# Re-dealing the first batch's k features and masked v between VectorE and ScalarE, with dummy matmuls up to the KV sums

## The chip, the cores and the metric

One core of a Trainium2 chip runs the whole program. The metric is the device time of one execution in microseconds (us). A profiled execution also has a span, from its first to its last instruction; here the time is the span plus 1.8 us (300.69 and 298.9). A change counts as faster or slower from 2% on, which is 6 us here.

## The reference, cut to what matters

Linear attention ("cosformer") over 8 batches, 8 heads, 576 tokens, 64 columns, then a two-layer product with squared ReLU over all 4608 tokens:

```python
q_p = concat([relu(q) * cos_w, relu(q) * sin_w])     # the same for k: 128 features a head
kv  = einsum('bhsf,bhsd->bhfd', k_p, v)              # the "KV sums"
num = einsum('bhsf,bhfd->bhsd', q_p, kv)
x   = num / (einsum('bhsf,bhf->bhs', q_p, k_p.sum(2)) + 1e-6)
out = relu(x @ w_in)**2 @ w_out                      # 512 -> 2048 -> 512
```

## The kernel before: the parts concerned

The products with w1 (`w_in`) and w2 (`w_out`) fill TensorE for most of the time. Only the head of the program, until batch 0's x exists, leaves TensorE free; it then proceeds in slots, in which attention of the next batches is woven into the products. k and v of batch 0 come over SyncE's queue, nine tokens a partition (`J9 = 9`), two halves of the heads in even and odd partitions. v is therefore copied twice per head, masked by half (`half_of`), to bf16 (`v9`, on VectorE, ScalarE or GpSimd):

```python
def of_half(eng, dst, src, g):
    if eng is nc.scalar:
        eng.activation(out=dst, in_=src, func=ACTF.Copy, scale=half_of[:, g : g + 1])
    else:
        eng.tensor_scalar_mul(out=dst, in0=src, scalar1=half_of[:, g : g + 1])
...
with tc.manual_schedule():
    for nm, h0, h1 in (("k", 0, 2), ("k", 2, 4), ("v", 0, 2), ("v", 2, 3), ("v", 3, 4)):
        load_nine(nm, h0, h1, nc.sync)
    load_qa(nc.sync)
    ...
    warm(26)                                  # dummy matmuls
    for h in range(HH):
        k9_dve(h, cos_col, 0)                 # VectorE: k cosine features
    k9_act(0, 2)                              # ScalarE: sines of heads 0 and 1
    k9_dve(2, sin_col, D)
    for g in range(2): v9(dve, 0, g)
    k9_dve(3, sin_col, D)
    for g in range(2): v9(act, 1, g)
    v9(nc.gpsimd, 2, 1, J9 - 1, J9)           # GpSimd: 64 elements; the loads below queue behind it
    load_w1(0, 4); load_qb(nc.gpsimd)         # w1, w2: cast to bf16 on the way, in quarters
    for i in range(1, 4): load_w1(i, 4)
    load_batch(1, nc.gpsimd, "q")
    load_w2(0, 4)
    load_batch(1, nc.gpsimd, "kv"); load_tail("q", 0, nc.gpsimd)
    for i in range(1, 4): load_w2(i, 4)
    ...
    for h in range(HH):
        kv9(h)                                # KV sums, TensorE
        if h == 1: kvz_copy(act, 0, 0, kzs[0][0][:, 0])
        if h > 1:  fill(4)                    # dummy matmuls
    qa_feat(0); kvz_copy(dve, 0, 1, kzs[0][1][:, 0]); qa_feat(1)
    ...
```

(cuts are marked; some short loops are set on one line). All loads by GpSimd are one stream in program order, and its place in GpSimd's program, behind a piece of masked v, is what sets its start. In batch 0's product with w2 each of 16 row blocks is used by four matmuls in turn, so the second quarter of w2 is first read by the 17th matmul.

Of the kernel before, what the change touches and what calls it, by code (L numbers as in the profile page):

```python
# [19 lines left out]
def kernel(  # L20
# [9 lines left out]
    nc = tc.nc  # L30
    P = nc.NUM_PARTITIONS
    B, H, S, D = q.shape
# [6 lines left out]
    J = S // P  # L39
# [24 lines left out]
    J9 = S // TAIL  # L64
    QA = J * TAIL

    def buf_of(nm, b):
        if (nm, b) not in kqv:
            kqv[nm, b] = inp.tile([P, HH * S * D // TAIL], F32, name=nm, tag=nm, bufs=2)
        return kqv[nm, b]  # L70
# [8 lines left out]
    def nine_of(nm):  # L79
        return buf_of(nm, 0).rearrange("p (h j d) -> p h j d", h=HH, j=J9)  # L80
# [24 lines left out]
    def load_rows(dst, src, n, h0, h1, eng):  # L105

        for g in range(2):
            eng.dma_start(  # L108
                out=dst.rearrange("(p g) h j d -> p g h j d", g=2)[:, g, h0:h1],
                in_=src[g * HH + h0 : g * HH + h1].rearrange("h (p j) d -> p h j d", j=n),  # L110
            )

    def load_nine(nm, h0, h1, eng):
        load_rows(nine_of(nm), srcs[nm][0], J9, h0, h1, eng)
# [19 lines left out]
    CA, CB, C9 = J + 1, 2 * J + 1, 2 * J + 3  # L134
    NC = C9 + J9
    cos_col = const.tile([P, NC], F32, name="cos_col")
    sin_col = const.tile([P, NC], F32, name="sin_col")
# [69 lines left out]
    vexts = att.tile([P, 2, J9 * HH, E1], BF16, name="vext")  # L207
# [14 lines left out]
    def vext_of(b, j):  # L222
        return vexts[:, b % 2, j * H : (j + 1) * H, :]

    def vext9(h):
        return vexts[:, :, h * J9 : (h + 1) * J9, :]

    def of_half(eng, dst, src, g):
        if eng is nc.scalar:
# [4 lines that stand above are left out]
    kps, kvzs, kzs, qps, tqs, qpTs, xs = {}, {}, {}, {}, {}, {}, {}  # L234
    nums, rdens, xts, xtails, xTs = {}, {}, {}, {}, {}

    def cached(tiles, key, shape, tag, bufs):
        if key not in tiles:
            tiles[key] = att.tile(shape, BF16, name=tag, tag=tag, bufs=bufs)
        return tiles[key]  # L240
# [8 lines left out]
    def kp9():  # L249
        t = cached(kps, 0, [P, J9 * HH, F], "kp", 1)  # L250
        return t.rearrange("p (h j) f -> p h j f", h=HH)
# [48 lines left out]
            nc.vector.tensor_copy(out=vext_of(b, j)[:, :, 0:D], in_=piece("v", b, j))  # L300


    def k9_dve(h, w, f0):
        nc.vector.scalar_tensor_tensor(  # L304
            out=kp9()[:, h, :, f0 : f0 + D],
            in0=nine_of("k")[:, h, :, :],
            scalar=0.0,
            in1=w[:, C9:NC].unsqueeze(2).to_broadcast([P, J9, D]),
            op0=ALU.max,
            op1=ALU.mult,  # L310
        )

    def k9_act(h0, h1):
        for j in range(J9):
            nc.scalar.activation(
                out=kp9()[:, h0:h1, j, D:F],
                in_=nine_of("k")[:, h0:h1, j, :],
                func=ACTF.Relu,
                scale=sin_col[:, C9 + j : C9 + j + 1],
            )  # L320

    def v9(eng, h, g, j0=0, j1=J9):
        of_half(eng, vext9(h)[:, g, j0:j1, 0:D], nine_of("v")[:, h, j0:j1, :], g)



# [1 line left out]
    def kv9(h):  # L328
        a, c = h // 2, h % 2 * 2 * E1
        if 0 not in kzs:  # L330

            kzs[0] = [
                ps_a.tile([P, 2, FP], F32, name="kz", tag="pa", bufs=1),
                ps_h.tile([P, 2, FP], F32, name="kzh", tag="hps", bufs=2),
            ]
            kvzs[0] = att.tile([P, H, E1], BF16, name="kvz", tag="kvz", bufs=2)
        for j in range(J9):
            nc.tensor.matmul(  # L338
                out=kzs[0][a][:, 0, c : c + 2 * E1].rearrange("p (g e) -> p g e", g=2),
                lhsT=kp9()[:, h, j, :],  # L340
                rhs=vext9(h)[:, :, j, :],
                start=(j == 0 and h % 2 == 0),
                stop=(j == J9 - 1 and h % 2 == 1),
            )

    def kvz_copy(eng, b, a, src):
        copy = eng.copy if eng is nc.scalar else eng.tensor_copy
        copy(
            out=kvzs[b].rearrange("p (g a h) e -> p a h g e", g=2, a=2)[:, a],
            in_=src[:, 0 : HH * E1].rearrange("p (h g e) -> p h g e", h=2, g=2),  # L350
        )

    def warm(n):

        wm = ps_h.tile([P, 2, FP], F32, name="wm", tag="hps", bufs=2)
        for i in range(n):
            nc.tensor.matmul(
                out=wm[:, i % 2, :], lhsT=zeros[:, 0:P], rhs=zeros[:, :], start=True, stop=True
            )

    def fill(n):

        w0 = HH * E1
        for i in range(n):
            nc.tensor.matmul(  # L365
                out=kzs[0][0][:, 0, w0:FP],
                lhsT=zeros[:, 0:P],
                rhs=zeros[:, 0 : FP - w0],
                start=True,
                stop=True,  # L370
            )
# [44 lines left out]
    def qa_feat(t, parts="cs"):  # L416
        for c in parts:
            f = feat_cos if c == "c" else feat_sin
            f(qpa(t), qa_of()[:, :, t, :], CA + t)

    def qa_T(t):
        tq = ps_y.tile([P, HH, P], BF16, name="tqa", tag="yps", bufs=2)
        tqs["a", t] = tq
        for h in range(HH):
            nc.tensor.transpose(tq[:, h, :], qpa(t)[:, h, :], ident[:, :])

    def qa_T_copy(t, eng):
        qpTs["a", t] = att.tile([P, HH, P], BF16, name="qpTp0", tag="qpTp0", bufs=5)
        copy = eng.copy if eng is nc.scalar else eng.tensor_copy
        copy(out=qpTs["a", t][:, :, :], in_=tqs["a", t][:, :, :])  # L430
# [288 lines left out]
    for j in (2, 3):  # L719
# [12 lines left out]
        k=(8, 8, 8, 9, 9),  # L732
        f=(4, 5, 6, 12, 13),
        kv=(10, 10),
        d=(11, 13, 15, 17, 21),
        t=(5, 6, 7, 16, 18),
# [5 lines left out]
        k=(26, 26, 27, 27, 28),  # L742
        f=(18, 20, 22, 26, 26),
        kv=(29, 29),
        d=(30, 31, 32, 33, 34),
# [3 lines left out]
        k=(31, 32, 33, 34, 35),  # L749
        f=(33, 33, 34, 34, 35),  # L750
        kv=(37, 38),
        d=(40, 41, 42, 43, 44),
    )
    for b in range(4, B):
        o, p = second[b - 2], first[b - 1]
# [4 lines left out]
            k=(o, o, o + 1, o + 1, o + 2),  # L760
            f=(o + 4, o + 4, o + 5, o + 5, o + 6),
            kv=(o + 3, o + 4),
            d=[p + 4 + j for j in range(NS)],
# [8 lines left out]
            rest()  # L772

    with tc.manual_schedule():
        for nm, h0, h1 in (("k", 0, 2), ("k", 2, 4), ("v", 0, 2), ("v", 2, 3), ("v", 3, 4)):
            load_nine(nm, h0, h1, nc.sync)
        load_qa(nc.sync)
        constants()
        ones_by_half()
        warm(26)  # L780
        dve, act = nc.vector, nc.scalar
        for h in range(HH):
            k9_dve(h, cos_col, 0)
        k9_act(0, 2)
        k9_dve(2, sin_col, D)
        for g in range(2):
            v9(dve, 0, g)
        k9_dve(3, sin_col, D)
        for g in range(2):
            v9(act, 1, g)  # L790

        v9(nc.gpsimd, 2, 1, J9 - 1, J9)
        load_w1(0, 4)
        load_qb(nc.gpsimd)
        for i in range(1, 4):
            load_w1(i, 4)
        load_batch(1, nc.gpsimd, "q")
        load_w2(0, 4)
        load_batch(1, nc.gpsimd, "kv")
        load_tail("q", 0, nc.gpsimd)  # L800
        for i in range(1, 4):
            load_w2(i, 4)
        load_batch(2, nc.gpsimd, "qkv")
        v9(act, 2, 0)
        v9(act, 2, 1, 0, J9 - 1)
        for g in range(2):
            v9(dve, 3, g)
        for h in range(HH):
            kv9(h)
            if h == 1:  # L810
                kvz_copy(act, 0, 0, kzs[0][0][:, 0])
            if h > 1:
                fill(4)
        qa_feat(0)
        kvz_copy(dve, 0, 1, kzs[0][1][:, 0])
        qa_feat(1)
        qa_T(0)
        qa_T_copy(0, dve)
        qa_feat(2)
        qa_T(1)  # L820
        qa_T_copy(1, dve)
        qa_feat(3)
        fill(2)
        qa_num(0)
        qa_T(2)
        qa_T_copy(2, act)
        fill(2)
        qa_num(1)
        qa_T(3)
        qa_T_copy(3, act)  # L830
        fill(3)
        att_div(0, 0)
        for t in (2, 3):
            qa_num(t)
        att_den(0, 1)
        for t, eng in enumerate((dve, act)):
            xa_T(t)
            xa_copy(t, eng)
        att_mul(0, 1)

        def second_pair():
            for t, eng in ((2, dve), (3, act)):
                xa_T(t)
                xa_copy(t, eng)
            for j in (2, 3):
                att_feat(0, j)

        run(0, {(0, 2): second_pair})
        for s in range(1, len(slots)):
            run(s)  # L850
# [28 lines left out]
```

## Time and profile before

| | before |
|---|---|
| time, median of 3 runs (range) | 301.3 us (300.77 to 301.48) |
| span of the profiled run | 298.9 us |
| TensorE busy | 97% |
| first product with w1 starts | 20.20 us |
| 17th product with w2 starts | 41.85 us |

The prediction shows the lines for this and how they are read.

### The profile page before, as it was taken

What the parts mean: (1) busy time and instruction counts of PE and PEld (TensorE: products, weight loads), DVE (VectorE), ACT (ScalarE), POOL (GpSimd) and SP (SyncE); (2) the same over time, 40 slices, a digit from 0 to 9 for tenths busy, and PEclk for the clock granted to TensorE, in tenths of its full rate; (3) what the DMA queues carried; (4) which work ended last, traced back from release to release, by engine and by line L of the source; (5) the groups of instructions that cost most, each with busy time, mean ns of one, the idle gap of its engine ahead of it and who ended that gap; (6) DMA issues with size and microseconds to landing.
All of it is one profiled execution on the core that took longest, in us unless ns stands there. A gap on an engine that the chain in (4) does not pass through costs nothing.

```text
span 298.9 us, 6467 instructions
## 1 busy us (share of the span) xinstructions
PE 289.2 (97%) x2655; PEld 204.2 (68%) x2677; DVE 144.6 (48%) x357; ACT 154.6 (52%) x229; POOL 50.3 (17%) x87
## 2 busy tenths in 40 slices
PE   8689999999999999999999999999999999999995
PEld 3569855889456984589655884589654884589544
DVE  3777674375649386238740387228740282033100
ACT  5636753666738564555554555555554552155311
POOL 1652504654121002000021001100021000100000
PEclk9799999999999999999999999999999999999999
DMA  6899993999999998799669937799679113100121
GB/s 207 231 235 278 336 203 81 331 329 257 196 195 170 161 311 131 216 199 321 160 154 209 317 62 91 231 185 323 162 158 209 39 35 82 71 35 2 35 72 70
DMA packets 74285, 52.98 MB, mean 177 GB/s; under 512 B 50832, under 2 KB 67984, under 8 KB 74256
## 3 DMA queue, kind: packets, MB, share of 16 engines
q1 hardware_dynamic: 64096, 28.84, 45.6%
q0 software_dynamic: 10016, 23.60, 29.2%
q8 instruction: 21, 0.34, 0.5%
q10 hardware_dynamic: 144, 0.13, 0.1%
q14 instruction: 8, 0.07, 0.1%
HBM read 36.70 MB, written 9.44 MB: 154 GB/s over the span
## 4 chain that ended last, share of the span: by engine, by line
PE 93%; DVE 2%; DMA 2%; ACT 1%; issue 1%; SPq 1%; ACTq 0%; DVEq 0%
PE hps L600 42%; PE yps L639 39%; PE num L514 3%; PE kz L385 2%; PE yh L639 2%; DMA k<-in_k_dram 2%; PE tq L491 1%; SPq L108 1%; PE kz L338 1%; PE kz L396 1%; PE kzh L338 1%; DVE kp L304 1%; PE tx L566 1%; DVE vext L232 1%; PE kz L365 0%
## 5 line engine op out<-in xcount | busy, mean ns | idle before, releaser
L600 PEld LDWEIGHTS <-w1sb 128*128 128x128 bf16 x1312 | 113.4, 98 | 12.7 <-issue 0.6
L600 PE MATMUL hps<-xT,w1sb 128*128 128x256 bf16 (+1 forms) x1056 | 118.3, 269 | 0.6 <-ACT xT L465 0.5
L639 PE MATMUL yps<-w2sb,gT 128*128 128x512 bf16 (+1 forms) x476 | 107.7, 372 | 1.2 <-DVE qpTp L500 0.2
L608 ACT ACTIVATE rt<-hps 128x1024 bf16<-128x1024 f32 x72 | 73.7, 1024 | 57.6 <-DVE gT L615 32.8
L639 PEld LDWEIGHTS <-gT 128*128 128x128 bf16 x528 | 49.8, 98 | 52.7 <-DVE qpTp L500 0.7
L615 DVE TENSOR_TENSOR gT<-rt 128x1024 bf16<-128x1024 bf16 x64 | 44.0, 687 | 79.0 <-ACT rt L608 79.0
L635 POOL DMA_DIRECT2D out_dram<-ysb x36 | 21.0, 584 | 172.5 <-ACT ysb L621 168.0
L621 ACT COPY ysb<-yps 128x512 f32<-128x512 f32 (+1 forms) x35 | 20.0, 575 | 54.0 <-PE yps L639 51.4
L287 ACT ACTIVATE qp<-q,sin_col 128x512 bf16<-128x512 f32 (+1 forms) x34 | 22.3, 693 | 7.5 <-DMA q<-in_q_dram 7.5
L535 DVE TENSOR_TENSOR x<-num,rden 128x512 bf16<-128x512 f32 x32 | 22.1, 691 | 1.1
L287 ACT ACTIVATE kp<-k,sin_col 128x512 bf16<-128x512 f32 (+1 forms) x35 | 21.5, 670 | 0.0
L277 DVE TENSOR_SCALAR qp<-q,cos_col 128x512 bf16<-128x512 f32 (+1 forms) x34 | 15.3, 485 | 11.5 <-DMA q<-in_q_dram 11.5
L528 DVE TENSOR_SCALAR den<-num 128x8 f32<-128x8 f32 (+1 forms) x40 | 6.6, 165 | 22.5 <-PE num L514 21.7
L277 DVE TENSOR_SCALAR kp<-k,cos_col 128x512 bf16<-128x512 f32 (+1 forms) x35 | 15.9, 453 | 0.0
L600 PE MATMUL hps<-xTt,w1sb 128*128 128x128 bf16 x256 | 15.3, 219 | 0.0
L639 PE MATMUL yps<-w2sb,gTt 128*128 128x512 bf16 x64 | 14.5, 379 | 0.0
L514 PEld LDWEIGHTS <-qpT 128*128 128x128 bf16 (+1 forms) x240 | 10.3, 100 | 3.3 <-issue 1.7
L300 DVE CAST vext<-v 128x512 bf16<-128x512 f32 x28 | 11.8, 421 | 0.0
L514 PE MATMUL num<-kvz,qpT 128*128 128x65 bf16 (+1 forms) x240 | 11.7, 194 | 0.0
L639 PEld LDWEIGHTS <-gTt 128*128 128x128 bf16 x64 | 6.3, 98 | 7.5
L385 PEld LDWEIGHTS <-kp 128*128 128x128 bf16 x224 | 8.5, 97 | 2.4
L639 PE MATMUL yh<-w2sb,gT 128*128 128x512 bf16 x30 | 9.1, 379 | 0.1
(80 smaller groups left out, 153.9 us busy)
## 6 DMA issues: line engine op xcount, KB each, us to landing
out_dram<-ysb POOLq DMA_DIRECT2D x26, 256.0 KB, 4.2
k<-in_k_dram SPq DMA_DIRECT2D x4, 1024.0 KB, 6.5
v<-in_v_dram SPq DMA_DIRECT2D x4, 1024.0 KB, 7.5
q<-in_q_dram SPq DMA_DIRECT2D x4, 1024.0 KB, 6.4
q<-in_q_dram POOLq DMA_DIRECT2D x3, 1024.0 KB, 9.9
k<-in_k_dram POOLq DMA_DIRECT2D x3, 1024.0 KB, 10.3
v<-in_v_dram POOLq DMA_DIRECT2D x3, 1024.0 KB, 10.7
w1sb<-in_moe_w_in_dram POOLq DMA_DIRECT2D x4, 512.0 KB, 9.1
```

The lines of the kernel that those rows point to most:

```text
L277: nc.vector.tensor_scalar(out=dst[:, :, 0:D], in0=src, scalar1=0.0, scalar2=cos_col[:, c : c + 1], op0=ALU.max, op1=ALU.mult,)
L287: nc.scalar.activation(out=dst[:, :, D:F], in_=src, func=ACTF.Relu, scale=sin_col[:, c : c + 1])
L300: nc.vector.tensor_copy(out=vext_of(b, j)[:, :, 0:D], in_=piece("v", b, j))
L385: nc.tensor.matmul(out=kz[:, a, c0 : c0 + E1], lhsT=kp_of(b, j)[:, h, :], rhs=vext_of(b, j)[:, h, :], start=(j == 0 and c == 0 and g == 0) ...
L514: nc.tensor.matmul(out=out, lhsT=lhsT, rhs=kvz[:, half * HH + hh, :], start=True, stop=True)
L535: nc.vector.tensor_tensor(out=x_of(b, j).rearrange("p (b k) (l d) -> p b k l d", b=n, l=2), in0=n4[:, :, :, 0:D].rearrange("p b (k l) d -> ...
L600: nc.tensor.matmul(out=out, lhsT=w1sb[:, kb, hb * P : (hb + 1) * P], rhs=rhs, start=(kb == 0), stop=(kb == KB - 1),)
L608: nc.scalar.activation(out=rt[:, :, :], in_=hps[:, :, :], func=ACTF.Relu)
L615: nc.vector.tensor_tensor(out=dst, in0=rt[:, :, :], in1=rt[:, :, :], op=ALU.mult)
L621: nc.scalar.copy(out=ysb[:, c0:c1], in_=acc)
L635: eng.dma_start(out=dst, in_=ysb[p0 : p0 + n, c0:c1])
L639: nc.tensor.matmul(out=acc, lhsT=lhsT, rhs=w2sb[:, hb, c0:c1], start=(hb == 0), stop=(hb == HB - 1))
```

## The change

Its intent: VectorE and ScalarE share k and v more evenly and in larger instructions, so that the KV sums start and end sooner; TensorE runs dummy matmuls right up to them, so that its clock is not lowered; batch 0's query features are computed before the KV sums end. The core of the diff (helpers that only gain an argument are cut):

```diff
-        for nm, h0, h1 in (("k", 0, 2), ("k", 2, 4), ("v", 0, 2), ("v", 2, 3), ("v", 3, 4)):
-            load_nine(nm, h0, h1, nc.sync)
+        for nm in "kv":
+            for h in (0, 2):
+                load_nine(nm, h, h + 2, nc.sync)
...
-        warm(26)
+        warm(34)
...
         k9_act(0, 2)
-        k9_dve(2, sin_col, D)
-        for g in range(2):
-            v9(dve, 0, g)
-        k9_dve(3, sin_col, D)
-        for g in range(2):
-            v9(act, 1, g)
-
-        v9(nc.gpsimd, 2, 1, J9 - 1, J9)
+        k9_act(2, 4, 5)
+        v9(dve, 0, 2, 0)
+        v9(act, 0, 2, 1, 0, 2 * J9 - 2)
+
+        v9(nc.gpsimd, 0, 2, 1, 2 * J9 - 2, 2 * J9)
         load_w1(0, 4)
...
-        v9(act, 2, 0)
-        v9(act, 2, 1, 0, J9 - 1)
-        for g in range(2):
-            v9(dve, 3, g)
+        for h in (2, 3):
+            k9_dve(h, sin_col, D, 5)
+        v9(dve, 2, 4, 0)
+        v9(act, 2, 4, 1)
         for h in range(HH):
             kv9(h)
             if h == 1:
                 kvz_copy(act, 0, 0, kzs[0][0][:, 0])
-            if h > 1:
-                fill(4)
-        qa_feat(0)
-        kvz_copy(dve, 0, 1, kzs[0][1][:, 0])
-        qa_feat(1)
...
+        for t in range(J):
+            qa_feat(t, "c")
+        for t in range(2):
+            qa_feat(t, "s")
+        kvz_copy(act, 0, 1, kzs[0][1][:, 0])
...
```

GpSimd's piece of masked v, ahead of its loads, is now 128 elements of heads 0 and 1, instead of 64 of head 2.

More of the change, by code (lines that the diff above doesn't have):

```diff
@@ L223, in vext_of, with vext9 @@
         return vexts[:, b % 2, j * H : (j + 1) * H, :]
-    def vext9(h):
-        return vexts[:, :, h * J9 : (h + 1) * J9, :]
+    def vext9(h0, h1):
+        return vexts[:, :, h0 * J9 : h1 * J9, :]
     def of_half(eng, dst, src, g):
@@ L300, in att_v, with k9_dve @@
             nc.vector.tensor_copy(out=vext_of(b, j)[:, :, 0:D], in_=piece("v", b, j))
-    def k9_dve(h, w, f0):
+    def k9_dve(h, w, f0, j0=0):
         nc.vector.scalar_tensor_tensor(
-            out=kp9()[:, h, :, f0 : f0 + D],
-            in0=nine_of("k")[:, h, :, :],
+            out=kp9()[:, h, j0:J9, f0 : f0 + D],
+            in0=nine_of("k")[:, h, j0:J9, :],
             scalar=0.0,
-            in1=w[:, C9:NC].unsqueeze(2).to_broadcast([P, J9, D]),
+            in1=w[:, C9 + j0 : NC].unsqueeze(2).to_broadcast([P, J9 - j0, D]),
             op0=ALU.max,
@@ L311, in k9_dve, with k9_act @@
         )
-    def k9_act(h0, h1):
-        for j in range(J9):
+    def k9_act(h0, h1, j1=J9):
+        for j in range(j1):
             nc.scalar.activation(
@@ L320, in k9_act, with v9 @@
             )
-    def v9(eng, h, g, j0=0, j1=J9):
-        of_half(eng, vext9(h)[:, g, j0:j1, 0:D], nine_of("v")[:, h, j0:j1, :], g)
+    def v9(eng, h0, h1, g, i0=0, i1=2 * J9):
+        src = nine_of("v")[:, h0:h1].rearrange("p h j d -> p (h j) d")
+        of_half(eng, vext9(h0, h1)[:, g, i0:i1, 0:D], src[:, i0:i1, :], g)
     def kv9(h):
@@ L340, in kv9 @@
                 lhsT=kp9()[:, h, j, :],
-                rhs=vext9(h)[:, :, j, :],
+                rhs=vext9(h, h + 1)[:, :, j, :],
                 start=(j == 0 and h % 2 == 0),
@@ L811 @@
                 kvz_copy(act, 0, 0, kzs[0][0][:, 0])
-            if h > 1:
-                fill(4)
-        qa_feat(0)
-        kvz_copy(dve, 0, 1, kzs[0][1][:, 0])
-        qa_feat(1)
-        qa_T(0)
-        qa_T_copy(0, dve)
-        qa_feat(2)
-        qa_T(1)
-        qa_T_copy(1, dve)
-        qa_feat(3)
+        for t in range(J):
[3 more added lines that the diff above has]
+        kvz_copy(act, 0, 1, kzs[0][1][:, 0])
+        for t in range(2):
+            qa_T(t)
+            qa_T_copy(t, dve)
+        for t in (2, 3):
+            qa_feat(t, "s")
         fill(2)
```

## The prediction

> **What bounds the kernel now.** I read the page first, for which engine fills the span, then the granted clock, then the chain that ended last over the first 45 us, and last the timeline of GpSimd, which issues the weight loads. Page, busy shares and slices of 7.5 us:
>
> ```profile
> PE 289.2 (97%) x2655; PEld 204.2 (68%) x2677; DVE 144.6 (48%) x357; ACT 154.6 (52%) x229; POOL 50.3 (17%) x87
> ...
> PE   8689999999999999999999999999999999999995
> ...
> DMA  6899993999999998799669937799679113100121
> ```
>
> TensorE is busy in all slices but the first three, so the change, which touches only the first 20 us, can gain only what it moves TensorE's later work forward. The DMA row says that the transfers are as full as TensorE until slice 20: that is the danger. The stretches of the head (columns PE, PEld, DVE, ACT, POOL busy, then granted clock, DMA share and rate):
>
> ```profile
> 10.00:11.00 1.00, 0.00 (x0) 0.00 (x0) 1.00 (x3) 1.00 (x2) 0.91 (x2) 1.00 0.98 320
> ...
> 12.00:13.00 1.00, 1.00 (x12) 1.00 (x11) 1.00 (x2) 0.04 (x1) 1.00 (x2) 0.50 0.54 39
> 13.00:14.00 1.00, 1.00 (x11) 0.94 (x9) 0.37 (x2) 1.00 (x3) 1.00 (x3) 0.50 1.01 164
> ```
>
> TensorE ends its warm matmuls at 8.61, idles 2.45 us, and from 11.4 to 14.8 us works at clock 0.50, just in the KV sums. The chain (start, us, what):
>
> ```profile
> 9.48 1.54 DVE vext L232 x2
> 11.02 0.04 issue
> 11.06 1.87 PE kz L338 x18
> 12.93 0.97 PE kzh L338 x9
> 13.90 0.84 PE kz L365 x4
> 14.74 0.62 PE kzh L338 x9
> 15.38 0.43 DVE kvz L348
> ...
> 20.20 0.61 PE hps L600 x8
> ...
> 41.55 0.43 PE yps L639 x2
> 41.99 0.46 PE yh L639 x2
> ```
>
> The masked v of VectorE releases the KV sums at 11.06; they end at 15.4; the first product with w1 starts at 20.20. Now the loads that GpSimd issues (start, us of issue, what, and what it waited for):
>
> ```profile
> 9.95 0.45 POOL L232 TENSOR_SCALAR vext<-v,half_of 128x64 bf16<-128x64 f32 x1 [8.02 <-DMA v<-in_v_dram]
> 10.48 0.96 POOL L191 DMA_DIRECT2D w1sb<-in_moe_w_in_dram  x1
> ...
> 12.36 2.27 POOL L191 DMA_DIRECT2D w1sb<-in_moe_w_in_dram  x3
> ...
> 20.46 0.63 POOL L92 DMA_DIRECT2D k<-in_k_dram  x1 [1.35 <-DMA w1sb<-in_moe_w_in_dram]
> ...
> 35.35 2.24 POOL L198 DMA_DIRECT2D w2sb<-in_moe_w_out_dram  x3 [2.44 <-DMA k<-in_k_dram]
> ```
>
> From its tenth transfer on GpSimd waits before an issue for the landing of the one eight before it: the stream runs as fast as transfers land, with a DMA share of 1.0 to 1.26 from 13 to 45 us. Landings, as issue plus time to landing: quarters of w1 at 10.48+5.7 = 16.2, 20.2, 23.6 and 13.82+12.3 = 26.1; q for token slots 2 and 3 at 11.44+6.5 = 17.9; the second quarter of w2 at 35.35+6.5 = 41.85. Its first user is the 17th matmul of the product with w2. The third was at 39.01, one takes 0.2165, so it is due at 41.83, and the timeline has it at 41.85, with the chain's piece after it 0.46 instead of 0.43. **This load has no slack.** Quarters 2, 3 and 4 of w1 have 3.1, 1.7 and 1.4 us (users at 23.30, 25.29, 27.50).
>
> **What the Trainium skill says.** (1) "TensorE: Matmul & The Clock Gate", section "What's actually happening": after an idle window of about 3.4 us the array gets half its clock, and a busy one gives it back. The trace agrees in kind: 0.50 for about 3.4 us, though the idle stretch was only 2.45. (2) "VectorE: DVE Perf Modes", section "What auto-detection actually checks": a one-source op in SBUF gets two results a cycle if the outermost dimensions of source and destination are both even, or equal. The trace agrees for even ones: v as 8 x 64 takes 421 ns (batch 1), while the masked copy of one head here, 9 x 64, takes 804. (3) "SBUF — State Buffer", section "Who interferes with whom": VectorE in such a two-port mode and GpSimd take turns at a shared port; the loser waits for the whole instruction. The trace hints at it: query features of 128x256 on VectorE take 344 ns alone and 560 at 15.73, while GpSimd issues. (4) "ScalarE: Activation LUTs", section "What ACT_TABLE_LOAD costs": 186 ns + 0.833 ns an element, 93 more for a pointer operand. Exact here: 386 ns measured at 128, 759 against 764 at 576.
>
> **The change part by part.**
> - Masked v on VectorE: four of 804 ns go, two of 18 x 64 = 1152 come. By (2) they run at two a cycle: the fixed part is 479 - 267 = 212 ns (feature of 512 at 479, 256 cycles at 0.96 GHz), so 600 + 212 = 0.81 us each, the price of one before.
> - k sine features on VectorE: two of 750 ns shrink to 4/9 of their elements. Two-source, 1.04 ns an element: 750 - 320*1.04 = 0.42 each.
> - VectorE: k cosine ends 8.90, v of two heads lands 8.97; v pair 9.05 to 9.86, k sine to 10.6, second v pair (landing about 10.4, estimated from 10.84 before with two issues fewer) to 11.4. Before: 13.1.
> - ScalarE: nine k instructions to 7.6 as before, five more at 0.304 pace to 9.15, v of 1024 elements 1.13 to 10.3, v of 1152 1.24 to 11.4.
> - Eight more warm matmuls at 0.21 = 1.7: TensorE is busy to about 10.3, just where the KV sums can start, with no idle stretch. At full clock one of 130 columns costs 130/2.4 = 54 ns, about 57 (the 65-column ones run at a pace of 31), so 18 take 1.03 instead of 1.87. Heads 2 and 3 start at 11.5 and end at 12.6; the eight fills between (0.84 us in the chain) are gone. KV ends **2.8 us earlier**.
> - Query features ahead of KV end: VectorE's four cosines 11.4 to 12.8, ScalarE's first two sines to 12.8, last KV copy 13.2. The first query product starts near 13.4 instead of 16.96, the first product with w1 near 16.3 instead of 20.20. Compute gives **3.9 us** at that point, and w1's first quarter (16.2) just suits.
>
> **What is left of it.** TensorE then meets the stream: w1 quarters at 20.2, 23.6, 26.1 cut the lead to 1.4 at the fourth, and the zero-slack quarter of w2 cuts it to nothing at 41.85, apart from d, by which the stream itself starts earlier. The stream starts after GpSimd's masked v. That now needs v of heads 0 and 1 (8.97) instead of head 2 (9.8): 0.8 earlier. But it has 128 elements instead of 64 (some 0.1 us more), and VectorE's two-port v pair is released by the same transfer; VectorE has started 0.1 us after a landing so far, GpSimd 0.15, so VectorE probably has the port first, and GpSimd would run 9.9 to 10.4 and issue w1 at 10.5, as before. So d = 0.7 if GpSimd is first, about -0.05 if not, and the descriptors of w1 may lose 0.1 to 0.3 more to the second v pair. At 2 to 1 for VectorE: 0.33*0.6 - 0.67*0.2, about **0.1**. After 42 us TensorE has no wait over 0.2 us, so what remains there lasts to the end.
>
> **Rivals.**
> - A: the stream does not bind (the match at 41.85 is chance, or earlier work of the engines lets transfers go faster). Then the lead of 1.4 from w1's fourth quarter, or more, stays: 299.5 to 300. For it: the delay seen at 41.85 is only 0.02 us. Against: landing and due time agree to 0.02, and the DMA share is over 1.
> - B: the port goes against GpSimd throughout, w1 is issued 0.5 later than before, and the kernel is slower: 301.8. For it: VectorE has two-port work from 9.05 to 12.9 nearly without a break. Against: GpSimd's issues near such work lost only some 0.06 us (0.82 against 0.76).
> - C: TensorE, early and waiting for w1, idles long enough to fall to half clock again. My stretches of idleness are under 1.5 us, so it is unlikely; it would cost up to 1.7 us, of which 1.2 is hidden before 41.85: 301.8.
> - D: v pairs don't reach two results a cycle: 1.4 us each, KV ends at 13.7 still 1.7 earlier, and GpSimd has its port: 300.5.
>
> **Range and chances.** Main line 301.3 - 0.1 = 301.2 (0.6), A 299.7 (0.2), D 300.5 (0.1), B and C 301.8 (0.1): mean 300.9; I say 301.0. The runs before spread 0.7 us, so 299.6 to 302.0. Two per cent is 6 us, more than the whole head can give: within 2% at 0.985.
>
> **What would show it.** Clock 1.00 in every stretch up to 20 us; VectorE's v pairs near 0.81 us; KV end near 12.6; first product with w1 near 16.3; new waits of TensorE before w1's second to fourth quarter and one of over 1 us before the second quarter of w2, whose landing moves by the whole gain and no more. GpSimd's masked v stretched or late shows who had the port. The prediction is wrong if TensorE does not wait there, or if the stream moves by over 1 us either way.

## More of the kernel before

One more line of the page belongs here, the shares of the engines in the chain of work that ended last; to be compared later:

```profile
PE 93%; DVE 2%; DMA 2%; ACT 1%; issue 1%; SPq 1%; ACTq 0%; DVEq 0%
```

TensorE (PE) makes up almost the whole chain, and transfers (DMA) only the 2% of the first load of k. The zero slack of w2's second quarter that the prediction finds is not visible in it.

## The result, and the profile after

| | before | changed |
|---|---|---|
| time, median of 4 runs (range) | 301.28 us (300.77 to 301.48) | 302.23 us (301.94 to 303.05) |
| ratio | | 1.0038, 95% interval 1.0015 to 1.0062 |
| span of the profiled run | 298.9 us | 300.3 us |

The ratio, here and below, is the mean time of one kernel's fast runs over that of the other's in the same rounds, so it is not quite the ratio of the medians quoted. The change makes the kernel about 1 us slower: within 2%, clear of the noise, and just above the range predicted (302.0).

The changed kernel's page, in order the busy tenths of TensorE and the engines' shares of the chain that ended last:

```profile
PE   8889979999999999999999999999999999999995
...
PE 83%; DMA 12%; SPq 1%; POOL 1%; issue 1%; ACT 0%; DVE 0%; POOLq 0%; ACTq 0%
```

The head itself is fuller (the second slice was 6), but the chain is now transfers for 12% of the span, some 36 us, and GpSimd (POOL) has come into it. The stretches from 11 to 14 us (us; PE, PEld, DVE, ACT, POOL busy; granted clock, DMA share, GB/s):

```profile
11.00:12.00 1.00, 1.00 (x19) 1.00 (x17) 1.00 (x2) 0.72 (x1) 1.00 (x2) 1.00 0.28 96
12.00:13.00 1.00, 0.60 (x12) 0.51 (x10) 0.43 (x2) 1.00 (x3) 1.00 (x2) 1.00 0.01 3
13.00:14.00 1.00, 1.00 (x21) 1.00 (x19) 1.00 (x3) 0.77 (x3) 1.00 (x2) 1.00 0.93 23
```

The clock stays at 1.00, as intended. But look at the last two columns: from 12 to 13 us almost nothing is transferred (3 GB/s). SyncE's loads are done and GpSimd's do not move data yet. The timeline shows why (start, us, engine, line, operation):

```profile
9.78 1.15 ACT L230 ACTIVATE vext<-v,half_of 128x1024 bf16<-128x1024 f32 x1 [0.46 <-DMA v<-in_v_dram]
9.79 0.82 DVE L232 TENSOR_SCALAR vext<-v,half_of 128x1152 bf16<-128x1152 f32 x1 [0.61 <-DMA v<-in_v_dram]
9.90 1.44 POOL L232 TENSOR_SCALAR vext<-v,half_of 128x128 bf16<-128x128 f32 x1 [7.97 <-DMA v<-in_v_dram]
10.53 0.85 DVE L304 SCALAR_TENSOR_TENSOR kp<-k,sin_col 128x256 bf16<-128x256 f32 x2
...
11.30 0.82 DVE L232 TENSOR_SCALAR vext<-v,half_of 128x1152 bf16<-128x1152 f32 x1
11.30 1.12 POOL L191 DMA_DIRECT2D w1sb<-in_moe_w_in_dram  x1
```

VectorE's pair of heads takes 0.82 us for 1152 elements, the price of 576 before. GpSimd, released by the same transfer 0.11 us later, needs 1.44 us for its 128 elements, and issues w1 at 11.30, 0.82 later than in the trace of before; the issue itself takes 1.12 instead of 0.96. TensorE's timeline in the changed kernel:

```profile
18.11 0.61 PE L602 MATMUL hps<-xT,w1sb 128*128 128x128 bf16 x8 [0.46 <-ACT xT L467]
...
22.26 1.92 PE L602 MATMUL hps<-xT,w1sb 128*128 128x256 bf16 x16 [0.89 <-DMA w1sb<-in_moe_w_in_dram]
...
27.40 1.92 PE L602 MATMUL hps<-xT,w1sb 128*128 128x256 bf16 x16 [0.21 <-DMA w1sb<-in_moe_w_in_dram]
...
43.23 0.59 PE L641 MATMUL yh<-w2sb,gT 128*128 128x512 bf16 x2 [1.33 <-DMA w2sb<-in_moe_w_out_dram]
```

The faster head gives a lead of 2.1 us at the first product with w1 (18.11 against 20.20). Waits for w1 take all but 0.1 of it by 27.40 (27.50 before), and at 43.23 TensorE has waited 1.33 us for w2's second quarter and starts 1.38 later than before. The spans differ by 1.4.

### The profile page after: what moved, and what is told of

The parts are those of the page before. It is cut to its first block, busy times and chain, and to the rows that moved or that the text cites. A ratio compares the mean times of both kernels' runs of the same rounds, so it can differ in the third digit from the quotient of the medians.

```text
span 300.3 us, 6464 instructions
## 1 busy us (share of the span) xinstructions
PE 289.8 (97%) x2655; PEld 203.2 (68%) x2677; DVE 143.1 (48%) x354; ACT 156.5 (52%) x233; POOL 51.9 (17%) x87
## 3 DMA queue, kind: packets, MB, share of 16 engines
HBM read 36.70 MB, written 9.44 MB: 154 GB/s over the span
## 4 chain that ended last, share of the span: by engine, by line
PE 83%; DMA 12%; SPq 1%; POOL 1%; issue 1%; ACT 0%; DVE 0%; POOLq 0%; ACTq 0%
PE yps L641 38%; PE hps L602 37%; DMA k<-in_k_dram 6%; PE num L516 3%; PE kz L387 2%; DMA q<-in_q_dram 2%; DMA w2sb<-in_moe_w_out_dram 2%; DMA v<-in_v_dram 2%; PE yh L641 2%; SPq L108 1%; PE kz L398 1%; POOL vext L232 0%; PE tx L568 0%; POOL w1sb L191 0%; ACT rt L610 0%
## 5 line engine op out<-in xcount | busy, mean ns | idle before, releaser
L359 PE MATMUL wm<-zeros 128*128 128x512 bf16 x34 | 9.9, 464 | 1.2 <-DVE odd L162 1.2
```

The lines of the kernel that those rows point to most:

```text
L359: nc.tensor.matmul(out=wm[:, i % 2, :], lhsT=zeros[:, 0:P], rhs=zeros[:, :], start=True, stop=True)
```

## The experiments

Theory: **GpSimd's stream of loads sets the end**, through the landing of w2's second quarter; the change delays the stream, because VectorE's two-port instruction (two results a cycle; points 2 and 3 of what the prediction takes from the skill) holds a port that GpSimd needs. Rivals: the stream's delay is chance, or due to GpSimd's larger piece; the loss arises elsewhere; the head's own pace or clock sets the end. Twelve kernels ran, in three calls of four on one chip each. The times of the kernel before in them were 301.44, 301.6 and 301.58 (medians of 11 runs each), so kernels of different calls are best compared by their ratios to it.

**1. The kernel before, again.** No edit.

> The kernel before, unchanged, for a second trace. If the later landing of v of heads 0 and 1 in the changed kernel (about 9.7 us against 9.0) is the chance of one execution, this trace should land somewhere between 8.9 and 9.7; if the way v is loaded causes it, 9.0 again. The second quarter of w2 should land within 0.1 us of when its first user is due, as before (41.8).

Measured: one run of 301.51, span 299.7. GpSimd's timeline, then TensorE's:

```profile
10.65 0.45 POOL L232 TENSOR_SCALAR vext<-v,half_of 128x64 bf16<-128x64 f32 x1 [8.72 <-DMA v<-in_v_dram]
11.19 0.96 POOL L191 DMA_DIRECT2D w1sb<-in_moe_w_in_dram  x1
```

```profile
42.70 0.59 PE L639 MATMUL yh<-w2sb,gT 128*128 128x512 bf16 x2 [0.65 <-DMA w2sb<-in_moe_w_out_dram]
```

v's second load took 5.6 us from issue to landing, against 4.8 in the first trace; in the other traces of both kernels and all variants it took 5.0 to 5.7. **The trace on which the prediction rests was an early execution.** This one, whose time lies close to the medians of the kernel before, issues w1 at 11.19 and already waits 0.65 us for w2's second quarter: its slack is below zero. My second expectation, landing within 0.1 us of when it is due, failed. Against this trace the changed kernel issues w1 only 0.1 us later.

**2. The first pair of masked v on VectorE as two single heads** (not in the two-port mode):

```diff
-        v9(dve, 0, 2, 0)
+        for h in (0, 1):
+            v9(dve, h, h + 1, 0, 0, J9)
```

> The changed kernel, but the first pair of masked v on VectorE as two instructions of one head (9 x 64, so not in the two-port mode). Port theory: GpSimd's masked v, 1.44 us in the changed kernel, falls to about 0.55, w1 is issued 0.8 to 0.9 us earlier, the second quarter of w2 lands as much earlier, and the time is about 301.4 (0.8 below the changed kernel's 302.2), although VectorE is 0.8 us longer busy. Rival (GpSimd is slow because its op has 128 elements, or because v is late): GpSimd's op stays over 1.2 us and the time stays at 302.2.

Measured: 300.96 us (300.52 to 301.33), ratio to before 0.9981 (0.9967 to 0.9995). VectorE and GpSimd:

```profile
9.56 1.54 DVE L232 TENSOR_SCALAR vext<-v,half_of 128x576 bf16<-128x576 f32 x2
```

```profile
9.67 0.61 POOL L232 TENSOR_SCALAR vext<-v,half_of 128x128 bf16<-128x128 f32 x1 [7.74 <-DVE kp L304]
10.24 0.96 POOL L191 DMA_DIRECT2D w1sb<-in_moe_w_in_dram  x1
```

VectorE needs 1.54 us in place of 0.82 for the same v, GpSimd's piece falls from 1.44 to 0.61, w1 is issued 1.06 earlier, and the kernel is 1.2 us faster than the changed one (302.12 in experiment 5; the ratios to before give 1.2 too), where 0.8 was expected: making VectorE slower makes the kernel faster. The number of elements is the same, so the larger piece is not the cause, and 0.61 is near the 0.55 that the port theory gave. VectorE's second pair now starts at 11.68, after the first issue of w1 has ended, so this run tests both effects of the port together, on GpSimd's piece and on the issue.

**3. The second quarter of w2 not waited for** (batch 0 reads the first quarter twice; wrong result):

```diff
-            out=acc, lhsT=lhsT, rhs=w2sb[:, hb, c0:c1], ...
+            rhs=w2sb[:, hb - 4 if b == 0 and 4 <= hb < 8 else hb, c0:c1], ...
```

> The changed kernel with a wrong result on purpose: batch 0 uses the first quarter of w2 in place of the second. Theory that the landing of w2's second quarter sets the end: TensorE's wait of 1.33 us there goes, and the time falls to about 300.9 to 301.2, close to the kernel before, since w1's fourth quarter, landing 1.3 us later than before, still holds TensorE to within 0.1 us of its old place. Rival (the loss arises elsewhere, or a wait of the same length follows): 302.2.

Measured: 300.35 us (300.18 to 300.92), ratio 0.9966 (0.9953 to 0.9979). TensorE's 17th product with w2:

```profile
41.45 0.59 PE L641 MATMUL yh<-w2sb,gT 128*128 128x512 bf16 x2
```

The wait is gone, and the time falls by 1.8 us against the changed kernel of experiment 5 (1.7 by the ratios), somewhat more than the 1.0 to 1.3 expected: the lead that w1's quarters leave TensorE was larger than I thought against a usual execution of before. GpSimd's piece still took 1.45 us in this trace. So the whole loss passes through this one landing.

**4. GpSimd gated on k instead of v.** No masked v on GpSimd; a copy of one element a partition, which waits for k of heads 2 and 3, stands ahead of the loads:

```diff
-        v9(act, 0, 2, 1, 0, 2 * J9 - 2)
+        v9(act, 0, 2, 1)
-        v9(nc.gpsimd, 0, 2, 1, 2 * J9 - 2, 2 * J9)
+        gate = const.tile([P, 1], F32, name="gate")
+        nc.gpsimd.tensor_copy(out=gate, in_=nine_of("k")[:, 3, J9 - 1, D - 1 : D])
```

> The changed kernel without masked v on GpSimd (ScalarE does those 128 elements too); in its place a copy of one element a partition that waits for k of heads 2 and 3. Stream theory: w1 is issued near 8.0 instead of 11.3, the stream lands some 2.5 to 3.3 us earlier, TensorE keeps the lead that its faster head gave (2.1 us at the first product with w1, less what v loses to the earlier stream), and the time is 299 to 300. Rival (the stream is bound by bandwidth that k, v and q take first, so that an earlier issue lands no earlier): 301.5 to 302.5.

Measured: median 301.13 us, but 299.49 to 302.65; ratio 0.9987 (0.9959 to 1.0015), so nothing can be claimed of the mean. The trace is of the fastest run: w1 issued at 8.24, the 17th product with w2 at 40.61, span 297.7. The stream theory holds in that run, and the median misses its range.

> A second look at the changed kernel gated on k, whose six runs spread from 299.5 to 302.7 and whose one trace is of the fastest. If w1, issued before v has landed, takes bandwidth from v in some executions, a slower one should show v of heads 2 and 3 or q landing later than in the trace of the fastest (11.5 and 12.9 us) and the KV sums with them. If the head is the same and only the landing of w2's second quarter moves, the spread is in the stream itself.

Measured: 301.28 in one run, span 299.5. The head is the same as in the faster trace (first product with w1 at 18.08 against 18.18), but k landed 0.8 us later, w1 was issued at 9.08, and w2's second quarter came 1.8 us later (17th product at 42.42). The spread is in the stream, as the second alternative said. Why it loses 1.0 us more than its later issue is open.

**5. The changed kernel, again**, beside the next three:

> The changed kernel, unchanged, beside the variants of this call: 302.0 to 302.5. GpSimd's masked v should again take about 1.4 us, w1 be issued near 11.3, and TensorE wait over 1 us before the second quarter of w2. If the 1.44 us were the chance of one execution, it would be about 0.6 here.

Measured: 302.12 us (302.03 to 302.36), ratio 1.0021 (1.0006 to 1.0035). GpSimd's piece took 1.45 us, w1 was issued at 11.29 in 1.32 us, TensorE waited 1.52 us and started the 17th product at 43.52. In all five traces with this head (the changed kernel twice, experiments 3, 7 and 9) GpSimd's piece took 1.44 to 1.45 us, so it is not chance.

**6. GpSimd gated on VectorE's last k cosine features**, otherwise as in 4:

```diff
+        nc.gpsimd.tensor_copy(out=gate, in_=kp9()[:, 3, J9 - 1, D - 1 : D])
```

> The changed kernel without masked v on GpSimd; GpSimd copies one element a partition of the k features that VectorE ends last (near 9.0), so w1 is issued near 9.4, after k has landed and shortly before v does. Stream theory: 1.8 to 1.9 us earlier than in the changed kernel, the second quarter of w2 lands near 41.4, the time is about 300.3 to 300.7. Unlike the gate on k itself it should not spread by 3 us, if that spread came from w1 taking bandwidth from v. Rival (the spread comes from another cause): 299.5 to 302.6 again.

Measured: 300.81 us (five runs 300.24 to 301.18, one 302.4), ratio 0.9982 (0.9961 to 1.0004). w1 was issued at 10.42, not 9.4: k landed late in this execution, and the copy of a single element took 0.80 us, since it started 0.05 us after VectorE's two-port pair (9.62 to 10.44). The time is just above my range, and the spread is smaller than in 4 but not gone.

**7. The two loads of batch 0's q tail moved behind w2's second quarter:**

```diff
-        load_tail("q", 0, nc.gpsimd)
-        for i in range(1, 4):
+        load_w2(1, 4)
+        load_tail("q", 0, nc.gpsimd)
+        for i in range(2, 4):
             load_w2(i, 4)
```

> The changed kernel with the two small loads of batch 0's q tail moved from before to after the second quarter of w2; nothing in the head changes. If that landing sets the end, the 128 KB less ahead of it bring it forward by 0.5 to 0.8 us and the time falls as much, to about 301.6. If the end is set elsewhere: 302.2.

Measured: 301.54 us (301.28 to 301.82), ratio 1.0000 (0.9985 to 1.0015), 0.6 below the changed kernel, as expected. Nothing in the head was touched, so only the order in the stream can have given it.

**8. Experiments 6 and 7 together:**

> Both of the last two edits together. If both work on the same landing, their gains add: 299.7 to 300.1, below the kernel before, and TensorE's wait before the second quarter of w2 shrinks to about 0.7 us. If the faster head can no longer gain (another bound in the head), it stays at 300.5.

Measured: 300.41 us (299.87 to 300.68), ratio 0.9960 (0.9944 to 0.9975). The gains add in time but for 0.2 us, yet the time is above the 299.7 to 300.1 expected. The wait did not shrink as I expected: it was 1.65 us, so TensorE had more lead than the stream could use. The gate's copy took 0.18 us here, before the v pair; then the first issue of w1 took 1.38 us. It had begun 0.25 us before the pair, and the pair was not lengthened:

```profile
9.35 1.38 POOL L191 DMA_DIRECT2D w1sb<-in_moe_w_in_dram  x1
9.60 0.82 DVE L232 TENSOR_SCALAR vext<-v,half_of 128x1152 bf16<-128x1152 f32 x1 [0.44 <-DMA v<-in_v_dram]
```

**9. The dummy matmuls back to 26** in the changed kernel, `warm(26)` for `warm(34)`:

> The changed kernel with 26 dummy matmuls again in place of 34. TensorE idles from 8.6 to 11, the clock falls to 0.5 for about 3.4 us in the KV sums, they end some 0.9 us later and so does the first product with w1 (near 19.2). If the stream of transfers sets the end, TensorE only waits less for w1's second quarter, and the time stays at 302.0 to 302.4. If the head sets it: 303.

Measured: 301.93 us (301.38 to 302.2), ratio 1.0012 (0.9997 to 1.0027), just below the 302.0 to 302.4 expected. The stretches as above:

```profile
12.00:13.00 1.00, 1.00 (x12) 0.90 (x10) 0.39 (x2) 0.85 (x3) 1.00 (x2) 0.50 0.00 1
13.00:14.00 1.00, 1.00 (x12) 1.00 (x11) 1.00 (x3) 0.78 (x2) 1.00 (x2) 0.50 0.74 46
```

TensorE idled 2.25 us and ran at half clock; the first product with w1 came at 18.76, about half a microsecond later. It cost nothing: the wait for w2 was 1.53 us. A real defect of the head was mended by the change, and in this kernel nothing came of it.

**10. The kernel before, with GpSimd's 64 elements taken from head 1** instead of head 2:

```diff
-        for g in range(2):
-            v9(act, 1, g)
-        v9(nc.gpsimd, 2, 1, J9 - 1, J9)
+        v9(act, 1, 0)
+        v9(act, 1, 1, 0, J9 - 1)
+        v9(nc.gpsimd, 1, 1, J9 - 1, J9)
...
-        v9(act, 2, 1, 0, J9 - 1)
+        v9(act, 2, 1)
```

> The kernel before with one edit: the 64 elements that GpSimd masks are of head 1 instead of head 2, so it waits for the v of heads 0 and 1, which lands about 0.7 us sooner. VectorE is in no two-port mode there, so GpSimd's op should keep 0.45 us and w1 be issued 0.7 us sooner. TensorE's wait before the second quarter of w2 (0.65 us in the second trace of before) should go, and the time fall from 301.5 to about 301.0; no further, since there the engines' own work is due. If the stream matters only in the changed kernel: 301.5.

Measured: 300.98 us (300.63 to 301.25), ratio 0.9982 (0.9967 to 0.9996). The wait for w2 was gone, and the time fell by 0.6 us, to 301.0 as expected. One detail failed. VectorE and GpSimd:

```profile
9.33 0.75 DVE L304 SCALAR_TENSOR_TENSOR kp<-k,sin_col 128x576 bf16<-128x576 f32 x1
```

```profile
9.58 0.83 POOL L232 TENSOR_SCALAR vext<-v,half_of 128x64 bf16<-128x64 f32 x1 [7.64 <-DMA v<-in_v_dram]
10.36 0.96 POOL L191 DMA_DIRECT2D w1sb<-in_moe_w_in_dram  x1
```

GpSimd's 64 elements took 0.83 us instead of 0.45, beside an instruction of VectorE that has two inputs in SBUF. In experiment 4 the copy of one element did the same: 0.75 and 0.76 us, started 0.05 us after such an instruction, against 0.18 in experiments 8 and 11 with none beside it. It is not only the two-port mode that holds GpSimd up.

**11. A version from what was learned:** the gate of 6, the order of 7, and the single heads of 2.

> The changed kernel with the gate on VectorE's k features, the q tail after w2's second quarter, and the first v pair as two instructions of one head, so that no two-port work stands beside the issue of w1's first quarter (1.38 us in the version without this). The issue should fall to 0.9 to 1.0 us, the stream come 0.3 to 0.5 us earlier, and the time be 300.0 to 300.4. If the stream is by now held by bandwidth and not by GpSimd: 300.4 again.

Measured: median 299.57 us (299.22 to 301.45; four of six runs at most 299.63), ratio 0.9955 (0.9930 to 0.9980): clear of both kernels though within 2%, and below the range expected. The trace is of the fastest of the six runs. GpSimd, then TensorE:

```profile
9.32 0.18 POOL L794 CAST gate<-kp 128x1 f32<-128x1 bf16 x1 [7.38 <-DVE kp L304]
9.44 0.90 POOL L191 DMA_DIRECT2D w1sb<-in_moe_w_in_dram  x1
```

```profile
40.38 0.59 PE L641 MATMUL yh<-w2sb,gT 128*128 128x512 bf16 x2 [0.41 <-DMA w2sb<-in_moe_w_out_dram]
```

The lead of the changed head is now nearly all used: only 0.41 us of waiting are left.

**All traces in one table** (us; the last column is the difference of the two before it):

| trace | GpSimd's op ahead of the loads | w1 issued | first product with w1 | 17th product with w2 (waited) | span | span less 17th |
|---|---|---|---|---|---|---|
| before | 0.45 | 10.48 | 20.20 | 41.85 | 298.9 | 257.05 |
| before, again | 0.45 | 11.19 | 20.27 | 42.70 (0.65) | 299.7 | 257.00 |
| changed | 1.44 | 11.30 | 18.11 | 43.23 (1.33) | 300.3 | 257.07 |
| changed, again | 1.45 | 11.29 | 18.29 | 43.52 (1.52) | 300.6 | 257.08 |
| 2 single heads | 0.61 | 10.24 | 17.96 | 42.07 (1.53) | 299.2 | 257.13 |
| 3 w2 not waited for | 1.45 | 11.36 | 18.30 | 41.45 | 298.5 | 257.05 |
| 4 gate on k | 0.75 | 8.24 | 18.18 | 40.61 (0.64) | 297.7 | 257.09 |
| 4 second | 0.76 | 9.08 | 18.08 | 42.42 (1.93) | 299.5 | 257.08 |
| 6 gate on k features | 0.80 | 10.42 | 18.08 | 41.93 (1.45) | 299.0 | 257.07 |
| 7 order | 1.45 | 10.76 | 17.75 | 42.42 (1.06) | 299.5 | 257.08 |
| 8 gate and order | 0.18 | 9.35 | 17.75 | 41.83 (1.65) | 298.9 | 257.07 |
| 9 warm 26 | 1.45 | 11.22 | 18.76 | 42.98 (1.53) | 300.0 | 257.02 |
| 10 before, head 1 | 0.83 | 10.36 | 20.68 | 42.31 | 299.3 | 256.99 |
| 11 best | 0.18 | 9.44 | 18.17 | 40.38 (0.41) | 297.5 | 257.12 |

After the 17th product all kernels take 257.0 to 257.1 us. Whatever the head does, the time is when that product starts, plus a constant. The column "first product with w1" falls into two groups, 20.2 to 20.7 and 17.75 to 18.8, and says nothing about the time.

## Why the prediction was wrong, point by point

**What bounds the kernel: right.** The prediction said that the lead of a faster head meets GpSimd's stream, that w1's quarters cut it and that w2's second quarter cuts it to nothing "apart from d, by which the stream itself starts earlier". Experiment 3 and the last column of the table confirm it. Its cut by w1 was too small: at the fourth quarter 0.1 us of the lead was left (27.40 against 27.50), not 1.4, since the stream came later than in the first trace. (Slips: the matmul at 39.01, called the third, is the fourth; with 13 steps of 0.2165 the due time of 41.83 stands. The 344 ns cosine, called alone, ran at 13.03 while GpSimd issued w1, so it is no measure without an issue.)

**The parts of the change: most durations right, landings too early.** VectorE's pair took 0.82 for 0.81 predicted, its two k sines 0.85 for 0.84, and the clock stayed at 1.00; but 18 matmuls of the KV sums took 1.21, not 1.03. The KV sums ended at 13.8 instead of 12.6, and the first product with w1 came at 18.11 instead of 16.3. About 0.7 to 0.8 us of that is v landing at 9.7 instead of 8.97, which the first trace had shown by chance; later, VectorE waited 0.57 for q and took 1.81 for its four cosines, 1.4 predicted. As the lead was lost anyway, this missing 1.8 us did not matter.

**The step that failed: the size of d.** The prediction reads "At 2 to 1 for VectorE: 0.33*0.6 - 0.67*0.2, about **0.1**". (The sum as written gives 0.06.) Measured, d was -0.5 to -0.8. The mechanism is the one it names, GpSimd behind VectorE at a shared port, but both terms were mis-sized:
- The branch in which GpSimd is first, worth 0.6, never came: VectorE started first in all five traces of this head, and GpSimd's piece took 1.44 to 1.45 every time. The start order, which the profile of before suggested (a lead of 0.05 us) and which was then 0.10 to 0.11 us each time, was treated as a lottery.
- The branch in which VectorE is first was to cost 0.2. It costs 0.5 to 0.8 at the landing, against the usual trace of before (42.70; 43.23 and 43.52). Of this 0.1 is the later issue of w1, 0.16 to 0.36 the longer issue beside VectorE's second pair (1.12 and 1.32 against 0.96), and 0.25 to 0.35 arises in the stream after that. That last part is not explained and may be spread between executions: from the end of w1's first issue to the issue of w2's second quarter the two traces of before took 23.91 and 24.15 us, the two of the changed kernel 24.25 and 24.43.

With d at -0.5 to -0.8 the prediction's own sum gives 301.8 to 302.1. To that comes the starting point: against the early first trace of before the difference is 1.4, and the four runs timed first happened to give before 301.28, where the three later sets gave 301.44 to 301.6.

**Rivals.** B, given a chance within a tenth, is what came, with its "two-port work from 9.05 to 12.9 nearly without a break"; the argument held against it, that issues near such work lose only 0.06 us, was from short instructions of 344 ns and does not carry to one of 0.82. (Its "0.5 later" for the issue of w1 is 0.8 against the first trace of before and 0.1 against the second.) A fell: the stream does bind. C fell: no stretch at a lower clock. D fell: the pair does reach two results a cycle; had the first pair not, experiment 2 shows that the kernel would have been 1.2 us faster.

**The range.** Its upper end of 302.0 gave B's direction a tail of 0.8 us above the main line (301.2). With zero slack at one landing, that landing's own spread of 0.8 us between executions belonged into it as well.

**What stays open.** Why early-gated streams (4, 6, 11) now and then lose 1 to 3 us, and the 0.25 to 0.35 us above. No trace of the longest runs of 4, 6 and 11 was taken.

## What to carry to other kernels

When two chains meet, a gain in one of them is worth what the other has in slack: read the slack of each transfer at its first user, and take a second trace before calling a slack zero, since landings moved by 0.8 us from one execution to the next. Look for what starts a queue of loads: here one small GpSimd instruction ahead of it decided a microsecond, and a VectorE instruction made twice as efficient, placed beside it, lost more than it gained. A cheap gate on an earlier event and a better order of the loads used the head's lead that the change alone could not.

## What the Trainium skill lacked or had wrong

- "SBUF — State Buffer", section "Who interferes with whom": its rule, that VectorE's two-port mode shuts GpSimd out for a whole instruction, agrees with these runs where GpSimd computes (1.44 to 1.45 us beside it, 0.61 without), and so does its clause on two inputs in SBUF (0.83 against 0.45 us). That whoever issues first gets the port does not fit the issue of a transfer by GpSimd in these traces. The first issue of w1 took 0.90 to 0.96 us undisturbed. Where VectorE's pair began with it, it took 1.12 us, and where the pair began 0.17 to 0.25 us after it, 1.31 to 1.38; the pair kept its 0.82. Where the pair began 0.39 to 0.48 us after an issue (experiments 2, 3 and 8), the issue kept its length (0.93 to 0.96) and the pair took 1.03 to 1.11.
- "TensorE: Matmul & The Clock Gate", section "Why this matters for your kernels": it warns of idle gaps over about 3 us. Here gaps of 2.25, 2.27 and 2.45 us were enough for the granted clock to fall to 0.50, while a wait of 1.93 us (second look of experiment 4) left it at 1.00; what lies between, no run shows.
- "VectorE: DVE Perf Modes", section "What auto-detection actually checks": it allows two results a cycle also for equal outermost dimensions. The masked copy of one head, nine rows of 64 in both source and destination as written, took 804 ns, the price of one a cycle; 18 rows took 0.82 us. As the nine rows of the source lie without gaps and those of the destination don't, the instruction may not carry them as equal; no run tells.
- No page was found that gives the spread of a landing between executions: the same 288 KB load of v took 4.8 to 5.7 us from issue to landing over the traces.
